# A fused DFT mixing and attention kernel: the seventh PSUM bank as one tile, 17 columns in every value product, and another order of two matmuls in the slots

## The chip, the cores and the metric

The kernel runs on one core of a Trainium2 chip. A core has a matrix engine (TensorE, PE in the profile; its weight loads are listed apart as PEld), a vector engine (VectorE, DVE), an activation engine (ScalarE, ACT), a general engine (GpSimd, POOL) and a queue engine that issues most of the transfers here (SyncE, SP). Matmul results land in PSUM, eight banks of 128 partitions by 512 float32 values. Each engine takes its instructions in the order of its own queue, and engines wait for each other with semaphores. The metric is the device time of one execution in microseconds; the number that counts is the median of the runs.

## What is computed

```python
def reference(A_x, A_dft_seq_re, A_dft_seq_im, A_dft_hid_re, A_dft_hid_im, B_x, B_wqkv, B_wo, gate_w):
    def _A_ref(x, dft_seq_re, dft_seq_im, dft_hid_re, dft_hid_im):
        a = jnp.einsum("bsd,ed->bse", x, dft_hid_re)
        b = jnp.einsum("bsd,ed->bse", x, dft_hid_im)
        y = jnp.einsum("ts,bse->bte", dft_seq_re, a) - jnp.einsum("ts,bse->bte", dft_seq_im, b)
        return y

    def _B_ref(x, wqkv, wo):
        B, S, D = x.shape
        H = 32; Dh = D // H
        qkv = (lambda x, *d: x.transpose(*d))((x @ wqkv).reshape(B, S, 3, H, Dh), 2, 0, 3, 1, 4)
        q, k, v = qkv[0], qkv[1], qkv[2]
        scale = Dh ** -0.5
        scores = jnp.einsum("bhqd,bhkd->bhqk", q, k) * scale
        p = _softmax(scores, axis=-1)
        o = jnp.einsum("bhqk,bhkd->bhqd", p, v)
        return (lambda x, *d: x.transpose(*d))(o, 0, 2, 1, 3).reshape(B, S, D) @ wo

    x = A_x
    g = _sigmoid((x * gate_w).sum(-1, keepdims=True))
    a = _A_ref(x, A_dft_seq_re, A_dft_seq_im, A_dft_hid_re, A_dft_hid_im)
    b = _B_ref(x, B_wqkv, B_wo)
    return g * a + (1 - g) * b
```

There are 2048 tokens of 512 values and 32 heads of 16 values. The projections and the attention use the same x as the DFT branch, and all values are float32. The softmax subtracts the row maximum of the scores, so each score matrix is made twice here: once for its maxima, once for its exponentials.

## The kernel before

The work on PE falls into products of four kinds. The dense ones (projections, the two DFTs, the output projection) are split into a high and a low part of each operand, so that one float32 product is three products of the faster type. They accumulate in one bank named d. A dense product contracts over 128 rows; the kernel cuts it into two **half products** of 64 rows each, issued in line 469 through `Chain.mm`. A **maxima product** (`a_tile`, line 292, letter a) makes one 128 x 512 block of scores with queries on the partitions; DVE reduces it to the maxima of its rows (line 294). A **score product** (`scores`, line 795, letter s) makes a block with keys on the partitions, and ACT takes its exponential into the tile pt (line 796). Both contract over 64 rows, so a half product in one half of the array's rows can run beside a score or maxima product in the other half. A **value unit** (`pv`, line 843) is four products of pt with 16 value columns and a column of ones, each into 32 of the 128 partitions of one bank, the sums acc. The value products are plain float32, and the trace shows each of them as two records.

`segment` writes a stretch of PE's queue from a pattern, a string of slots. A slot such as `a5` puts a maxima product into bank 5, with a half product of the dense work in the other row half; `|` is a value unit. In this kernel the order of every queue is the order of the program, since the schedule is manual. Three patterns matter: THIN (the DFT along the hidden axis, 26 segments), FULL (the DFT along the sequence, 192 segments of 16 slots and two value units) and NINE (the output projection, 26 segments). Segments come in twos: the first issues the lower rows of 16 dense products, the second the upper rows of the same 16.

Banks: seven are numbered. s and a products rotate over banks 0 to 5 by the digits of the pattern; bank 6 holds the sums acc, and between two sums it also takes a product (`s6` in slot 5 and `a6` in slot 11 of FULL). The last value unit of a segment closes the sum (`close`): ACT copies acc to SBUF (`evacuate`, line 822) and POOL adds the copy to the running total (line 823). Before the change, the bank is then given up and a new tile acc is made by the next value unit, whose products take 32 columns so that all partitions of the new tile are written.

In slot 0 of a FULL segment the s or a product stands ahead of the half product in PE's queue (`first`); in the 15 other slots it stands behind it. A half product that opens a segment waits for the reader of the product in the last slot of the segment before, through `users`, which each half product empties.

Of the kernel before, what the change touches and what calls it, by code (L numbers as in the profile page):

```python
# [9 lines left out]
F32 = mybir.dt.float32  # L10
# [5 lines left out]
P = 128  # L16
# [6 lines left out]
NT = S // P  # L23
# [8 lines left out]
def mix_kernel(ctx: ExitStack, tc: tile.TileContext, xa_t, xa, wqkv, w_hid, w_seq, wo, gate_w, out):  # L32
# [5 lines left out]
    nc = tc.nc  # L38
# [29 lines left out]
    psO = Ring(6)  # L68
# [31 lines left out]
    acc = psO.tile([P, 512], F32, "acc")  # L100
# [86 lines left out]
    def bank():  # L187
        nonlocal banks
        banks += 1
        return (psS if banks % 2 else psA).tile([P, 512], F32, name="s" if banks % 2 else "a")  # L190


    with tc.tile_pool(name="qk", bufs=1, reuse_waits="tile") as pool:
# [38 lines left out]
        for tb in range(4):  # L232
# [4 lines left out]
            for c in range(2):  # L237
                if tb == 0 and c == 0:
                    pss = [bank() for _ in range(4)]
                    for kt in range(KT):  # L240
                        x = xab[tb][:, :, :, kt * P:(kt + 1) * P]
# [8 lines left out]
                for ct in range(4):  # L250
                    ps = bank()
# [34 lines left out]
    def a_tile(i, h, ps=None, bank=None):  # L286
        p, j = divmod(i, 64)
        qt, kb = divmod(j, 4)
        if ps is None:
            ps = psA.tile([P, 512], F32, "a", bank)  # L290
        r = slice(64 * h, 64 * h + (64 if p else 48))
        nc.tensor.matmul(ps, qs[p % 2][r, qt * P:(qt + 1) * P], ks[p % 2][r, kb * 512:(kb + 1) * 512],  # L292
                         start=True, stop=True)
        user = nc.vector.tensor_reduce(mx[p % 2][:, h, qt, kb:kb + 1], ps, AX.X, ALU.max)  # L294
        hf = j // 32
        a_left[p, hf] = a_left.get((p, hf), 64) - 1
        if not a_left[p, hf]:
            deferred.extend((partial(m_parts, p, hf), partial(m_rows, p, hf)))
        return user
# [111 lines left out]
    for s in range(8):  # L411
        ps = psS.tile([P, 512], F32, name="s")
# [369 lines left out]
    def scores(u, qb, h, bank=(psS, "s"), number=None):  # L782
        p, r = divmod(u, 32)
        hf, kt = divmod(r, 16)
        q0 = hf * 1024 + qb * 512
        if u >= UNITS - 16:

            blk, kt = divmod(kt, 8)
            q0, kt = 1024 + blk * 512, 2 * kt + qb
        if u not in pts:  # L790
            pts[u] = work.tile([P, 4, 512], F32, name="pt", bufs=4)
        pool, name = bank
        ps = pool.tile([P, 512], F32, name=name) if number is None else pool.tile([P, 512], F32, name, number)
        rr = slice(64 * h, 64 * h + (64 if p else 50))
        nc.tensor.matmul(ps, ks[p % 2][rr, kt * P:(kt + 1) * P], qs[p % 2][rr, q0:q0 + 512], start=True, stop=True)  # L795
        return nc.scalar.activation(pts[u][:, 2 * qb + h], ps, AF.Exp, bias=0.0, scale=DH ** -0.5)  # L796

    def pv_last(u):
        blk, k2 = divmod(u - UNITS + 16, 8)
        pt = pts.pop(u)  # L800
        for j in range(4):
            x, h = divmod(j, 2)
            nc.tensor.matmul(acc[32 * j:32 * j + 17], vt[:, 2 * k2 + x, NP - 1, 16 * h:16 * h + 17], pt[:, j],
                             start=k2 == 0, stop=k2 == 7)
        if blk == 0 and k2 == 7:
            last_pairs.append(LastPair(0, [(psS, "s"), (psA, "a")]))
            last_pairs[0].copy(1)

    part = []

    def evacuate(p, hf, done):

        nonlocal total
        if total is None:
            total = work.tile([P, 512], F32, name="oe", bufs=2)
            nc.scalar.copy(total, acc)
        else:
            if not part:
                two = work.tile([P, 2, 512], F32, name="part", tag="w15")
                part.extend(two[:, i] for i in range(2))  # L820
            part.reverse()
            nc.scalar.copy(part[0], acc)  # L822
            nc.gpsimd.tensor_tensor(total, total, part[0], ALU.add)  # L823
        if done:
            for qb in range(2):
                nc.sync.dma_start(o_d[hf][p, :, qb * 512:(qb + 1) * 512], total[64 * qb:64 * qb + 64])
            total = None

    def pv(u, close=False):
        nonlocal acc  # L830
        if u >= UNITS - 16:
            return pv_last(u)
        p, r = divmod(u, 32)
        hf, kt = divmod(r, 16)
        pt = pts.pop(u)
        begin, done, width = acc is None or kt == 0, kt == NT - 1, 17
        if acc is None:
            acc = psO.tile([P, 512], F32, "acc")
            width = 32
        v = vt.rearrange("p t n d -> p (t n d)")[:, 33 * (NP * kt + p):]  # L840
        for j in range(4):
            h = j % 2
            i = nc.tensor.matmul(acc[32 * j:32 * j + width], v[:, 16 * h:16 * h + width], pt[:, j],  # L843
                                 start=begin, stop=done or close)
        if done or close:
            evacuate(p, hf, done)
            if close:
                acc = None
        return i

    def take(gen, n, whole=True):
# [12 lines left out]
    def issue(x, half, stop=True):  # L864
        chain, st, mv, after, last = x
        i = chain.mm(st, mv, half, last and stop)
        if stop and after:
            after()
        return i
# [15 lines left out]
    for hf in range(2):  # L885
        for ct in range(4):
            n = 3 if hf and ct == 3 else 4
# [32 lines left out]
    FULL = "a5 s4 a2 s0 a3 s6 a5 s4 s1 s0 s2 a6 a3 a4 s5 a1 | |"  # L920
# [15 lines left out]
    users, valued, exponentials = [], 0, []  # L936

    def score(kind, h, number=None):
        x = next(streams[h][kind == "a"], None)
        if x:  # L940
            users.append((kind, a_tile(*x, bank=number) if kind == "a" else scores(*x, number=number)))
            if kind == "s":
                exponentials.append(users[-1][1])

    def values(close=False):
        nonlocal valued
        i = pv(valued, close)
        valued += 1
        return i

    def segment(pattern, half, ds, stop):


        nonlocal users, full_now
        full_now = pattern == FULL
        before, users = users, []
        ds, turned = iter(ds), False
        for n, slot in enumerate(pattern.split()):
            number, other = None, None
            if slot[1:2].isdigit():  # L960
                number, other = int(slot[1]), int(slot[3]) if slot[2:] else None
                slot = slot[::2]
            first = not n and pattern == FULL
            if slot == "|":
                end = n == len(pattern.split()) - 1
                i = values(end)
                if end and pattern == FULL:

                    tc.add_manual_dep(i.ins, exponentials[-2].ins.name,
                                      mybir.DependencyInfo(mybir.DependencyClass.Sync, mybir.DependencyReason.DATA))  # L970
                while between:
                    between.pop(0)()
                if deferred and pattern in NINE and not turned and "|" in pattern.split()[n + 1:]:
                    deferred.pop(0)()
                    turned = True
                continue
            if first:

                score(slot, 1 - half, number)
            if len(slot) == 1:  # L980
                x = next(ds, None)
                if x:

                    before = before if x[0].begun else None
                    i = issue(x, half, stop)
                    users = []
                    if before:
                        tc.add_manual_dep(
                            i.ins, dict(reversed(before)).get("s", before[0][1]).ins.name,
                            mybir.DependencyInfo(mybir.DependencyClass.Sync, mybir.DependencyReason.DATA))  # L990
                        before = None
            if slot != "-" and not first:
                score(slot[-1] if slot[0] == "+" else slot[0], 1 - half, number)
            if len(slot) == 2 and slot[0] != "+":
                score(slot[1].lower(), half, other)

        while full_now and deferred:
            deferred.pop(0)()
        if deferred and not (pattern in NINE and (turned or len(deferred) == 1)):
            deferred.pop(0)()  # L1000
# [11 lines left out]
    first = proj(0, (0, 1, 2), one * 5 + two[:1] + one, range(7))  # L1012
# [5 lines left out]
    pump(hid, 12)  # L1018
    ds = take(hid, 12)
    segment(START[0], 0, ds, False)  # L1020
    pump(hid, 12)
    segment(START[1], 1, ds, True)
    values()
    values(True)
    for patterns, ds in pairs():
        for half in range(2):
            run_plan(valued)
            pattern = FULL if patterns is FULL else patterns[half]
# [5 lines left out]
    for bank in (*three[:1], *three):  # L1034
        scores(*next(streams[1][0]), bank)
# [62 lines left out]
```

## Time and profile before

| | |
|---|---|
| median of 3 runs | 1665.3 us (1664.87 to 1665.42) |
| the profiled execution | 1664.94 us, span 1663.0 us |
| stage of the projections | 0 to 206 us |
| THIN segments | 206 to 353 us |
| FULL segments | 353 to 1458 us |
| NINE segments | 1458 to 1600 us |
| rest | 1600 to 1663 us |

The busy part of the page tells how long each engine worked and how many instructions it had. The chain of waits follows the work that ended last back through the program. Groups put together instructions of one line, engine and shape, with count, busy time, mean duration in nanoseconds, and the idle time ahead of them. The timeline lists instructions by start (us from the start of the span), duration in us, engine, line, operation, output <- inputs, shape and count; instructions of one kind that overlap are merged into one row. In a shape such as 64*128 64x512, the first pair is the rows and columns of the array in use, the second the operand that moves through it.

### The profile page before, as it was taken

Reading aid. Unit: us, or ns where it says so; the run is one execution under the profiler, and the core shown is the slowest. Engines: PE = TensorE matmul, PEld = TensorE weight load, DVE = VectorE, ACT = ScalarE, POOL = GpSimd, SP = SyncE. Lnnn points to the kernel's source line nnn. Section 1 sums busy time; section 2 is a strip of 40 time slices with the busy share of each in tenths; the row PEclk is TensorE's granted clock in tenths of the full one; section 3 lists DMA queues with packets and bytes.
Section 4 is the critical chain, followed back from the end, with each engine's and each line's share of the span. In section 5 each row is a group of like instructions: output and inputs, shape, how many; then the busy total and the mean of one; then the engine's idle time right before and its main releaser. Section 6 shows DMA issues by size and latency. Waiting matters only on the chain.

```text
span 1663.0 us, 34370 instructions
## 1 busy us (share of the span) xinstructions
PE 1655.0 (100%) x13040; PEld 1008.6 (61%) x13040; DVE 1382.6 (83%) x2361; ACT 1266.0 (76%) x2469; POOL 653.5 (39%) x615
## 2 busy tenths in 40 slices
PE   9999999999999999999999999999999999999998
PEld 7888855556566656665666656665566556644443
DVE  5439888888888888888888888888888888899954
ACT  5212388888888888888788888888788878889996
POOL 0202133443434455444343455544444456333330
PEclk9999999999999999999999999999999999999999
DMA  9973610414151343414157534315141535462114
GB/s 295 349 158 120 180 15 9 70 34 85 44 93 47 73 112 81 94 46 79 47 90 254 93 114 96 88 56 90 52 85 59 112 103 122 139 188 40 37 32 140
DMA packets 85245, 167.13 MB, mean 100 GB/s; under 512 B 22461, under 2 KB 22717, under 8 KB 81069
## 3 DMA queue, kind: packets, MB, share of 16 engines
q1 hardware_dynamic: 84648, 164.30, 39.5%
q8 instruction: 102, 1.67, 0.5%
q10 hardware_dynamic: 432, 0.66, 0.1%
q14 instruction: 63, 0.51, 0.1%
HBM read 109.67 MB, written 55.17 MB: 99 GB/s over the span
## 4 chain that ended last, share of the span: by engine, by line
PE 98%; DMA 1%; DVE 0%; POOL 0%; SPq 0%; issue 0%; DVEq 0%; ACT 0%; POOLq 0%; ACTq 0%
PE acc L843 28%; PE d L469 24%; PE a L292 17%; PE s L795 16%; PE s L383 3%; PE s L415 1%; PE d L383 1%; PE a L108 1%; PE s L108 1%; PE s L107 1%; PE a L107 1%; PE a L109 1%; PE s L109 1%; PE a L469 1%; PE s L469 0%; PE s L244 0%
## 5 line engine op out<-in xcount | busy, mean ns | idle before, releaser
L294 DVE TENSOR_REDUCE mx<-a 128x1 f32<-128x512 f32 x2026 | 1260.1, 683 | 172.8 <-PE a L292 144.5
L796 ACT ACTIVATE pt<-s 128x512 f32<-128x512 f32 x2006 | 1021.9, 623 | 33.7 <-PE s L795 17.6
L292 PE MATMUL a<-ks,qs 64*128 64x512 f32 (+1 forms) x2026 | 723.6, 407 | 0.0
L795 PE MATMUL s<-qs,ks 64*128 64x512 f32 (+1 forms) x2006 | 663.9, 395 | 1.0 <-DVE on L736 0.8
L469 PE MATMUL d<-xab,ch 64*128 64x512 f32 x2016 | 644.7, 394 | 0.0
L823 POOL TENSOR_TENSOR oe<-oe,part 128x512 f32<-128x512 f32 x215 | 278.0, 1293 | 660.5 <-ACT part L822 655.5
L292 PEld LDWEIGHTS a<-ks,qs 64*128 64x128 f32 (+1 forms) x2026 | 361.0, 184 | 212.3 <-issue 123.3
L843 PE MATMUL acc<-pt,vt 128*17 128x512 f32 (+1 forms) x3968 | 487.2, 599 | 0.0
L795 PEld LDWEIGHTS s<-qs,ks 64*128 64x128 f32 (+1 forms) x2006 | 361.4, 184 | 71.3 <-ACT pt L796 27.3
L469 PE MATMUL d<-xab,cl 64*128 64x512 f32 x1008 | 397.6, 394 | 0.0
L469 PEld LDWEIGHTS d<-xab,ch 64*128 64x128 f32 x2016 | 366.6, 184 | 28.0
L822 ACT COPY part<-acc 128x512 f32<-128x512 f32 x215 | 126.1, 587 | 187.2 <-PE acc L843 186.2
L843 PEld LDWEIGHTS acc<-pt,vt 128*17 128x17 f32 (+1 forms) x3968 | 92.9, 102 | 218.3 <-issue 138.9
L469 PEld LDWEIGHTS d<-xab,cl 64*128 64x128 f32 x1008 | 185.7, 184 | 14.3
L454 POOL TENSOR_TENSOR cl<-craw,ch 128x512 fp32r<-128x512 f32 x126 | 162.2, 1287 | 10.1
L469 PE MATMUL d<-wre,xab 64*128 64x512 f32 x336 | 90.3, 402 | 0.0
L469 PEld LDWEIGHTS d<-wre,xab 64*128 64x128 f32 x336 | 59.9, 184 | 40.2 <-issue 12.1
L453 POOL CAST ch<-craw 128x512 fp32r<-128x512 f32 x126 | 77.0, 611 | 17.3 <-PE s L795 10.2
L469 PE MATMUL d<-wo_hl,o_hl 64*128 64x512 f32 (+1 forms) x246 | 65.3, 397 | 0.0
L103 ACT CAST hl<-s 128x512 fp32r<-128x512 f32 x28 | 16.1, 587 | 58.4 <-PE s L383 31.3
L469 PEld LDWEIGHTS d<-wo_hl,o_hl 64*128 64x128 f32 (+1 forms) x246 | 44.2, 185 | 16.3 <-ACT pt L796 10.2
L383 PE MATMUL s<-wch,xab 64*128 64x512 f32 x192 | 41.3, 391 | 0.0
(171 smaller groups left out, 992.7 us busy)
## 6 DMA issues: line engine op xcount, KB each, us to landing
craw<-w_seq SPq DMA_DIRECT2D x128, 256.0 KB
qk<-hl SPq DMA_DIRECT2D x32, 512.0 KB
qs<-qk SPq DMA_DIRECT2D x96, 128.0 KB
ks<-qk SPq DMA_DIRECT2D x96, 128.0 KB
b<-hl SPq DMA_DIRECT2D x16, 512.0 KB
xab<-b SPq DMA_DIRECT2D x16, 512.0 KB
o<-oe SPq DMA_DIRECT2D x62, 128.0 KB
oh<-nh SPq DMA_DIRECT2D x12, 512.0 KB
```

The lines of the kernel that those rows point to most:

```text
L107: nc.tensor.matmul(ps, sh, mh, start=first, stop=False)
L292: nc.tensor.matmul(ps, qs[p % 2][r, qt * P:(qt + 1) * P], ks[p % 2][r, kb * 512:(kb + 1) * 512], start=True, stop=True)
L294: user = nc.vector.tensor_reduce(mx[p % 2][:, h, qt, kb:kb + 1], ps, AX.X, ALU.max)
L383: i = nc.tensor.matmul(ps, st[r], mv[r], start=not half and not j, stop=half == 1 and j == 11)
L453: nc.gpsimd.tensor_copy(h1, raw)
L454: nc.gpsimd.tensor_tensor(l1, raw, h1.bitcast(F32), ALU.subtract)
L469: i = nc.tensor.matmul(self.ps, st[r], mv[r], start=not self.begun, stop=stop)
L795: nc.tensor.matmul(ps, ks[p % 2][rr, kt * P:(kt + 1) * P], qs[p % 2][rr, q0:q0 + 512], start=True, stop=True)
L796: return nc.scalar.activation(pts[u][:, 2 * qb + h], ps, AF.Exp, bias=0.0, scale=DH ** -0.5)
L822: nc.scalar.copy(part[0], acc)
L823: nc.gpsimd.tensor_tensor(total, total, part[0], ALU.add)
L843: i = nc.tensor.matmul(acc[32 * j:32 * j + width], v[:, 16 * h:16 * h + width], pt[:, j], start=begin, stop=done or close)
```

## The change

All products into bank 6, also those of slots 5 and 11, now go to the one tile acc that is made at the start of the kernel. No new tile is made behind a closed sum, so every value product takes 17 columns; a flag `closed` tells the next value unit to begin a new sum. Partitions 17 to 31 of each 32 in acc then keep what the last s or a product left, and the copy takes them along; no later step uses them. In FULL segments the s or a product of slots 0 to 14 is issued ahead of the slot's half product; slot 15 keeps the half product first.

```diff
--- before.py
+++ after.py
@@ -790,7 +790,10 @@
         pool, name = bank
-        ps = pool.tile([P, 512], F32, name=name) if number is None else pool.tile([P, 512], F32, name, number)
+        if number == 6:
+            ps = acc
+        else:
+            ps = pool.tile([P, 512], F32, name=name) if number is None else pool.tile([P, 512], F32, name, number)
@@ -806,7 +809,7 @@
-    part = []
+    part, closed = [], False
@@ -827,25 +830,22 @@
     def pv(u, close=False):
-        nonlocal acc
+        nonlocal closed
...
-        begin, done, width = acc is None or kt == 0, kt == NT - 1, 17
-        if acc is None:
-            acc = psO.tile([P, 512], F32, "acc")
-            width = 32
+        begin, done = closed or kt == 0, kt == NT - 1
+        closed = False
         v = vt.rearrange("p t n d -> p (t n d)")[:, 33 * (NP * kt + p):]
         for j in range(4):
             h = j % 2
-            i = nc.tensor.matmul(acc[32 * j:32 * j + width], v[:, 16 * h:16 * h + width], pt[:, j],
+            i = nc.tensor.matmul(acc[32 * j:32 * j + 17], v[:, 16 * h:16 * h + 17], pt[:, j],
                                  start=begin, stop=done or close)
         if done or close:
             evacuate(p, hf, done)
-            if close:
-                acc = None
+            closed = close
         return i
@@ -938,7 +938,7 @@
-            users.append((kind, a_tile(*x, bank=number) if kind == "a" else scores(*x, number=number)))
+            users.append((kind, a_tile(*x, acc if number == 6 else None, number) if kind == "a" else scores(*x, number=number)))
@@ -960,7 +960,7 @@
-            first = not n and pattern == FULL
+            first = pattern == FULL and n < 15
```

On PE, the start of a FULL segment before the change: slots 0 to 5, with what each waits for (the names are output <- operands; L292 is a maxima, L795 a score, L469 a half product).

```order
L292 MATMUL a<-ks_975,qs_973 128x512 [waits Activation_49]
L469 MATMUL d<-xab_205,cl 128x512 [waits DVE_49]
L469 MATMUL d<-xab_205,ch 128x512
L795 MATMUL s<-qs_973,ks_975 128x512
L469 MATMUL d<-xab_205,ch 128x512
L292 MATMUL a<-ks_975,qs_973 128x512
L469 MATMUL d<-xab_205,cl 128x512
L795 MATMUL s<-qs_973,ks_975 128x512
L469 MATMUL d<-xab_206,ch 128x512
L292 MATMUL a<-ks_975,qs_973 128x512
L469 MATMUL d<-xab_206,ch 128x512
L795 MATMUL s<-qs_973,ks_975 128x512 [waits Activation_49]
```

The same place after the change (lines have moved by 3, and the score of slot 5 writes acc):

```order
L292 MATMUL a<-ks_974,qs_972 128x512 [waits Activation_49]
L469 MATMUL d<-xab_203,ch 128x512 [waits DVE_49]
L798 MATMUL s<-qs_973,ks_975 128x512
L469 MATMUL d<-xab_203,ch 128x512
L292 MATMUL a<-ks_974,qs_972 128x512
L469 MATMUL d<-xab_203,cl 128x512
L798 MATMUL s<-qs_973,ks_975 128x512
L469 MATMUL d<-xab_203,ch 128x512
L292 MATMUL a<-ks_974,qs_972 128x512
L469 MATMUL d<-xab_203,ch 128x512
L798 MATMUL acc<-qs_973,ks_975 128x512 [waits Activation_49]
L469 MATMUL d<-xab_203,cl 128x512
```

From slot 1 on, each pair has changed places; slot 0 is as it was.

The end of a FULL segment on PE before, slots 13 to 15 and the two value units:

```order
L469 MATMUL d<-xab_206,ch 128x512
L292 MATMUL a<-ks_975,qs_973 128x512 [waits Activation_49]
L469 MATMUL d<-xab_206,ch 128x512
L795 MATMUL s<-qs_973,ks_975 128x512 [waits DVE_49]
L469 MATMUL d<-xab_206,cl 128x512
L292 MATMUL a<-ks_975,qs_973 128x512 [waits Activation_49]
L843 MATMUL acc<-pt,vt 32x512 [waits DVE_49]
L843 MATMUL acc<-pt,vt 32x512 x3
L843 MATMUL acc<-pt,vt 17x512 x3
L843 MATMUL acc<-pt,vt 17x512 [waits Activation_49]
```

And after:

```order
L292 MATMUL a<-ks_974,qs_972 128x512 [waits Activation_49]
L469 MATMUL d<-xab_204,ch 128x512
L798 MATMUL s<-qs_973,ks_975 128x512 [waits DVE_49]
L469 MATMUL d<-xab_204,cl 128x512
L469 MATMUL d<-xab_204,ch 128x512
L292 MATMUL a<-ks_974,qs_972 128x512 [waits Activation_49]
L844 MATMUL acc<-pt,vt 17x512 [waits DVE_49]
L844 MATMUL acc<-pt,vt 17x512 x6
L844 MATMUL acc<-pt,vt 17x512 [waits Activation_49]
```

In slots 13 and 14 the waiting product now stands ahead of the half product of its slot, slot 15 is as before, and all value products take 17 columns. The order on DVE, POOL and SP is the same as before, and so is that on ACT, where the copy of the sums has a wait more:

```order
L822 COPY part<-acc 128x512 [waits PE_49,Pool_49]
L796 ACTIVATE pt<-s 128x512 [waits PE_49] x4
L796 ACTIVATE pt<-s 128x512 [waits PE_49,Activation_49]
L796 ACTIVATE pt<-s 128x512 [waits PE_49]
L796 ACTIVATE pt<-s 128x512 [waits PE_49,Activation_49]
```

```order
L825 COPY part<-acc 128x512 [waits DVE_49,PE_49,Pool_49]
L799 ACTIVATE pt<-s 128x512 [waits PE_49] x2
L799 ACTIVATE pt<-acc 128x512 [waits PE_49]
L799 ACTIVATE pt<-s 128x512 [waits PE_49]
L799 ACTIVATE pt<-s 128x512 [waits PE_49,Activation_49]
```

The first of these two is before the change, the second after it: the copy of the sums, then exponentials of the next segment.

## The prediction

> **What bounds the kernel now.** I read the page first: the busy shares and the chain that ended last.
>
> ```profile
> span 1663.0 us, 34370 instructions
> PE 1655.0 (100%) x13040; PEld 1008.6 (61%) x13040; DVE 1382.6 (83%) x2361; ACT 1266.0 (76%) x2469; POOL 653.5 (39%) x615
> PE 98%; DMA 1%; DVE 0%; POOL 0%; SPq 0%; issue 0%; DVEq 0%; ACT 0%; POOLq 0%; ACTq 0%
> ```
>
> TensorE (PE) is busy for the whole span and 98% of the chain is its own work, so a nanosecond that it gains in every segment is kept, as long as VectorE (DVE) and ScalarE (ACT) follow. The stage that the change edits most comes next, from the busy time by stretches: columns are PE, weight loads, DVE, ACT and POOL.
>
> ```profile
> 353.00:1458.00 1105.00, 1105.00 (x9224) 669.19 (x9216) 972.97 (x1664) 901.01 (x1762) 508.92 (x474) 1.00 0.39 90
> ```
>
> These 1105 us hold the 192 FULL segments, 5.755 us each. DVE works 88% of them and ACT 82%, so both can follow a PE that becomes a few tenths of a per cent faster. The granted clock is 1.00 throughout. I therefore look at what a segment's 5.755 us consist of, in PE's order of time, for one of average length.
>
> ```profile
> 698.76 0.50 PE L292 MATMUL a<-ks,qs 64*128 64x512 f32 x1
> 698.76 0.50 PE L469 MATMUL d<-xab,ch 64*128 64x512 f32 x1
> 699.09 0.39 PE L795 MATMUL s<-qs,ks 64*128 64x512 f32 x1
> 699.10 0.39 PE L469 MATMUL d<-xab,ch 64*128 64x512 f32 x1
> ...
> 700.02 0.39 PE L795 MATMUL s<-qs,ks 64*128 64x512 f32 x1
> ...
> 700.71 0.39 PE L469 MATMUL d<-xab,cl 64*128 64x512 f32 x1
> 700.71 0.39 PE L795 MATMUL s<-qs,ks 64*128 64x512 f32 x1
> ...
> 701.40 0.39 PE L292 MATMUL a<-ks,qs 64*128 64x512 f32 x1
> ...
> 701.64 0.39 PE L292 MATMUL a<-ks,qs 64*128 64x512 f32 x1
> ...
> 702.10 0.39 PE L795 MATMUL s<-qs,ks 64*128 64x512 f32 x1
> 702.30 0.39 PE L469 MATMUL d<-xab,ch 64*128 64x512 f32 x1
> 702.33 0.39 PE L292 MATMUL a<-ks,qs 64*128 64x512 f32 x1
> 702.65 1.92 PE L843 MATMUL acc<-pt,vt 128*32 128x512 f32 x16
> 704.51 0.49 PE L292 MATMUL a<-ks,qs 64*128 64x512 f32 x1
> ```
>
> The two row halves of the array work side by side: a half product d in one, a score or maxima product (I call both s here) in the other. Sixteen slots take 698.76 to 702.65, the two value units 702.65 to 704.51, and the next segment follows without a gap. Two things matter. In slot 1 the program issues d before s, and yet s starts first (699.09 against 699.10): the halves start on their own, whatever the order of issue. And from slot 8 on (700.71) d leads: seven steps later it is at 702.30, a step of 0.227 us, while s is at 702.33, a step of 0.231. The value units need all rows, so the later stream, s, sets their start.
>
> **Part 1: 17 columns in every value product.** Each first value unit behind a closed sum has four products of 32 columns, and the trace shows each in two passes. The groups with shapes kept apart:
>
> ```profile
> L843 PE MATMUL acc<-pt,vt 128*17 128x512 f32 x2008 | 261.4, 593 | 0.0
> L843 PE MATMUL acc<-pt,vt 128*32 128x512 f32 x1960 | 261.1, 605 | 0.0
> ```
>
> 1960 records are 1960 / 8 = 245 units. A wide product is 12 ns longer in the mean (605 against 593). That this is time of the stream, and not a longer overlap, is seen where a wide and a narrow unit stand alone between slots, in the stage ahead of the FULL segments:
>
> ```profile
> 313.01 1.05 PE L843 MATMUL acc<-pt,vt 128*17 128x512 f32 x8
> 314.00 0.49 PE L469 MATMUL d<-wre,xab 64*128 64x512 f32 x1
> ...
> 316.49 1.06 PE L843 MATMUL acc<-pt,vt 128*32 128x512 f32 x8
> 317.49 0.50 PE L292 MATMUL a<-ks,qs 64*128 64x512 f32 x2
> ```
>
> The narrow unit takes 0.99 us to the next slot, the wide one 1.00. So the term is 245 x 0.012 = 2.9 us gained. Its bounds are 0 (the rounded rows could hide a step of almost nothing) and 245 x 0.02 = 4.9 (the most that they allow).
>
> **Part 2: one tile for the seventh bank.** DVE, POOL and SP issue the same instructions in the same order, and the matmuls of this bank wait as before. What is new is that the copy of the sums on ACT waits for DVE too, because it now reads rows that the maxima product of slot 11 wrote. The value units ahead of that copy have waited for the same reduction already:
>
> ```profile
> 701.85 0.69 DVE L294 TENSOR_REDUCE mx<-a 128x1 f32<-128x512 f32 x1
> ...
> 702.65 0.15 PEld L843 LDWEIGHTS acc<-pt,vt 128*32 128x32 f32 x7 [0.31 <-DVE mx L294]
> ```
>
> The reduction ends at 702.54, 0.11 us ahead of the value units, and the copy comes behind them. I cost this at nothing. The 0.11 us is also the room by which the slots may shrink before DVE becomes the gate; and as that reduction starts when slot 11's product is done (701.40 + 0.39 = 701.79), it moves along with a faster PE. If ACT took time to test a third wait, it would be part of the last rival's cost.
>
> **Part 3: s ahead of d in slots 1 to 14.** Nothing is added: 14 pairs a segment swap places, in 192 segments. What can change is who leads. The row to compare with is a segment in which s stays ahead by chance:
>
> ```profile
> 1331.57 0.49 PE L292 MATMUL a<-ks,qs 64*128 64x512 f32 x1
> ...
> 1333.29 0.39 PE L795 MATMUL s<-qs,ks 64*128 64x512 f32 x1
> 1333.30 0.39 PE L469 MATMUL d<-xab,cl 64*128 64x512 f32 x1
> ...
> 1334.88 0.39 PE L795 MATMUL s<-qs,ks 64*128 64x512 f32 x1
> 1334.90 0.39 PE L469 MATMUL d<-xab,ch 64*128 64x512 f32 x1
> 1335.11 0.39 PE L292 MATMUL a<-ks,qs 64*128 64x512 f32 x1
> 1335.12 0.39 PE L469 MATMUL d<-xab,ch 64*128 64x512 f32 x1
> 1335.44 1.92 PE L843 MATMUL acc<-pt,vt 128*32 128x512 f32 x16
> 1337.29 0.50 PE L292 MATMUL a<-ks,qs 64*128 64x512 f32 x1
> ```
>
> From slot 7 to slot 14 the leading s steps by 0.227 us and the following d by 0.229, both reach slot 15 within 0.01, and from its start to the next segment's it takes 5.72 us where the average one took 5.75. That is 0.03 x 192 = 5.8 us, the upper bound of this part. s falls behind where it must wait for a bank, as its weight loads show:
>
> ```profile
> 700.03 0.18 PEld L292 LDWEIGHTS a<-ks,qs 64*128 64x128 f32 x1
> ...
> 701.67 0.18 PEld L292 LDWEIGHTS a<-ks,qs 64*128 64x128 f32 x1
> ...
> 702.16 0.18 PEld L292 LDWEIGHTS a<-ks,qs 64*128 64x128 f32 x1
> ```
>
> A load normally starts with the product before it. The load for slot 6 comes about 0.01 us late (700.03 against the product of slot 5 at 700.02), that for slot 13 0.03 late (701.67 against 701.64), that for slot 15 0.06 late (702.16 against 702.10). Slot 6 is where d passes s today, because d's loads stand ahead of the waiting one. With s first, d's load of the same slot is queued behind that wait, and d gets no free pass. What is queued behind a waiting s is now that d and all later products; the value units wait for both streams. But a load has room: for slot 15 it starts 0.17 us ahead of its product (702.16 to 702.33), where a full step is 0.23, and that product still came on time, so a load 0.06 late costs nothing. The waits of slots 6 and 13 lie within that. The low bound is therefore 0 when the waits still let the two streams drift apart, and, if the room were not there, a loss of (0.01 + 0.03) x 192 = 7.7 us. Slot 15, with the longest wait, keeps d first. I take half of the upper bound, 2.9 us: s will lead more often, but it is s that waits, and a segment led by s is nearer to what the swap makes than one in which d is held 0.04.
>
> The Trainium skill, in "TensorE: Matmul & The Clock Gate", section "The mechanism", says that matmuls start strictly in program order and only weight loads are pulled ahead. The pair at 699.09 and 699.10 speaks against this, since s started ahead of the d issued before it. By that rule d could never start ahead of its slot's s after the swap, but s would keep its own step of 0.231, the segment would end where it ends now, and only part 1 would be left, the time of the first rival.
>
> **The sum.** -2.9 (columns) + 0 (tile) - 2.9 (order) = -5.8 us. The profiled execution took 1664.94 us, of which the span is 1663.0; with 5.8 less it is 1659.1. The median of the runs, 1665.3, is 0.4 above that execution, which gives 1659.5.
>
> **The rivals.** (a) The order does nothing, since the halves start on their own and s is slow by its own waits, not by d. For it: slot 1 above. Against it: the leader's step is 0.227 in both segments, whichever stream leads. Time: 1665.3 - 2.9 = 1662.4. (b) The order gives all of its bound: s leads in nearly every segment, as at 1331.57. Against it: the waits of slots 13 and 15 remain, and a shorter slot stage makes ACT's releases later by comparison. Time: 1665.3 - 2.9 - 5.8 = 1656.6. (c) Slower: PE's queue stands behind s. At slots 6 and 13 s waits for DVE and ACT, d's load stands behind it and both halves idle, 0.04 us a segment that d's lead absorbed before. It decides where d's load starts more than 0.06 us after the product before it; then the time is 1665.3 - 2.9 + 7.7 = 1670.1. For it: DVE and ACT are 88% and 82% busy and the waits do occur in every segment. Against it: the room of 0.06 us, and the one segment led by s that shows no such loss.
>
> **How the numbers follow.** The forecast of 1659.5 has a chance of 0.4, (a) 0.28, (b) 0.2, (c) 0.12. About 0.2%, 3.3 us, is what a measurement of this kernel can tell from no change: that puts the line at 1662.0. (a) lies just on the other side of it, so it goes to the same side but for a small part; faster is 0.4 + 0.2 and I leave it at 0.6, same 0.28, slower 0.12. The range takes in (b) with 1 us below it and the near half of the way from no change to (c): 1655.5 to 1667. The likeliest case alone would be 1658 to 1661.
>
> **What would show it.** Part 1: no group of 32 columns is left, and the two units take 0.01 us less than the 1.86 us above (702.65 to 704.51). Part 2: ACT's copy starts no later behind the value units than before. Part 3: in most segments s starts ahead of d in the late slots, the step of s falls to 0.227 to 0.229, and the value units start less than 3.89 us after the segment's start. The forecast is wrong if the late d products start more than 0.03 behind s (then the lag has only changed sides), if d's loads at slots 6 and 13 come more than 0.06 late, or if the value units' loads start right at the end of the reduction of slot 11.

## The result and the profile after

The change takes 3.4 us off: 1661.83 us median (1661.07 to 1662.97, 17 runs) against 1665.26 us before (1664.09 to 1666.32, 17 runs). The ratio is 0.998, 95% interval 0.9973 to 0.9987. The forecast was 1659.5 in a range of 1655.5 to 1667; the time of the first rival, the columns without any gain from the order, was 1662.4.

The page of the profiled execution after the change, which took 1662.97 us:

```profile
span 1661.1 us, 34392 instructions
PE 1651.7 (99%) x13040; PEld 976.0 (59%) x13040; DVE 1383.3 (83%) x2361; ACT 1264.7 (76%) x2469; POOL 654.0 (39%) x615
PE 98%; DMA 1%; DVE 0%; POOL 0%; SPq 0%; ACT 0%; issue 0%; DVEq 0%; POOLq 0%; ACTq 0%
```

PE is still 98% of the chain. The groups, with shapes kept apart, hold one form of value product now, and ACT sat idle ahead of the copy of the sums, which has a third wait now, as long as before (185.7 us; the last row is that of before, 187.2 us). In the FULL segments the copy starts 0.137 us behind the recorded end of the last value product in the median, against 0.148 before:

```profile
L844 PE MATMUL acc<-pt,vt 128*17 128x512 f32 x3968 | 484.1, 596 | 0.0
L825 ACT COPY part<-acc 128x512 f32<-128x512 f32 x215 | 126.4, 588 | 185.7 <-issue 174.6 <-POOL cl L454 5.7 <-PE acc L844 5.1
```

```profile
L822 ACT COPY part<-acc 128x512 f32<-128x512 f32 x215 | 126.1, 587 | 187.2 <-PE acc L843 186.2 <-POOL ch L453 0.6
```

PE's timeline for a FULL segment of the length that most have after the change:

```profile
687.61 0.49 PE L292 MATMUL a<-ks,qs 64*128 64x512 f32 x1
687.61 0.49 PE L469 MATMUL d<-xab,cl 64*128 64x512 f32 x1
...
688.87 0.40 PE L798 MATMUL acc<-qs,ks 64*128 64x512 f32 x1
688.88 0.40 PE L469 MATMUL d<-xab,ch 64*128 64x512 f32 x1
...
689.57 0.39 PE L798 MATMUL s<-qs,ks 64*128 64x512 f32 x1
689.58 0.39 PE L469 MATMUL d<-xab,ch 64*128 64x512 f32 x1
...
691.18 0.39 PE L292 MATMUL a<-ks,qs 64*128 64x512 f32 x1
691.18 0.39 PE L469 MATMUL d<-xab,cl 64*128 64x512 f32 x1
691.50 1.91 PE L844 MATMUL acc<-pt,vt 128*17 128x512 f32 x16
693.35 0.49 PE L292 MATMUL a<-ks,qs 64*128 64x512 f32 x1
```

The value units take 1.85 us (691.50 to 693.35; 1.86 before). The order did what it says: s (score or maxima product) leads and d (half product) follows within 0.01 us up to slot 15 (691.18), where s was 0.03 behind before. Yet the sixteen slots take 3.89 us (687.61 to 691.50), as in the average segment before. From slot 8 to slot 15 the leading s needs 691.18 - 689.57 = 1.61, a step of 0.230; before, the leading d had 0.227. The lead of d is gone, and s has kept its pace. The prediction's other signs of being wrong did not come: the loads of the value units start 0.11 us behind the end of the reduction of slot 11 in the median (0.09 before), and d's loads of slots 6 and 13 start 0.014 and 0.010 us behind the product before them in the mean.

The rounded rows hide differences of a few ns, so I took the unrounded starts of the matmuls in the traces, one execution of each kernel, over all 192 FULL segments, and averaged. "Slots" is from a segment's first product to its first value product, "values" from there to the next segment, "lag" is how far s starts behind d in slot 15, "FULL" the time from the first segment's start to the last one's, in us like the rest. The experiments below are in the same table.

```
kernel                        slots    values   lag     FULL
before                        3.899    1.854    0.031   1098.87
after                         3.896    1.842   -0.001   1095.96
columns alone                 3.903    1.842    0.035   1097.13
order alone                   3.896    1.854    0.001   1098.37
half product first            3.918    1.842    0.051   1100.14
d first in 6, 13, 15          3.900    1.842    0.032   1096.55
maxima over 256               3.878    1.842   -0.003   1092.48
exponentials of 256           3.898    1.842   -0.004   1096.30
both of 256                   3.857    1.842   -0.005   1088.45
other banks                   3.879    1.842   -0.004   1092.57
other banks, old order        3.888    1.842    0.021   1094.25
other banks, d first in 13    3.875    1.842    0.008   1091.82
```

FULL gained 2.9 us: 191 x 0.0127 = 2.4 in the value units and 191 x 0.0025 = 0.5 in the slots. Another 0.4 us came in the THIN stage and behind FULL. The spans differ by 1.9 us only, because the profiled execution after the change reached the first dense product of line 107 1.3 us later (at 17.64 us against 16.30), ahead of any edited instruction.

### The profile page after: what moved, and what is told of

It is laid out like the page before. It is cut to its first block, busy times and chain, and to the rows that moved or that the text cites. A ratio compares the mean times of both kernels' runs of the same rounds, so it can differ in the third digit from the quotient of the medians.

```text
span 1661.1 us, 34392 instructions
## 1 busy us (share of the span) xinstructions
PE 1651.7 (99%) x13040; PEld 976.0 (59%) x13040; DVE 1383.3 (83%) x2361; ACT 1264.7 (76%) x2469; POOL 654.0 (39%) x615
## 4 chain that ended last, share of the span: by engine, by line
PE 98%; DMA 1%; DVE 0%; POOL 0%; SPq 0%; ACT 0%; issue 0%; DVEq 0%; POOLq 0%; ACTq 0%
PE acc L844 28%; PE a L292 21%; PE s L798 19%; PE d L469 12%; PE s L383 3%; PE acc L798 3%; PE acc L292 2%; PE s L415 1%; PE d L383 1%; PE a L108 1%; PE a L107 1%; PE s L108 1%; PE s L107 1%; PE a L109 1%; PE s L109 1%; PE a L469 1%
## 5 line engine op out<-in xcount | busy, mean ns | idle before, releaser
L294 DVE TENSOR_REDUCE mx<-a 128x1 f32<-128x512 f32 x1834 | 1144.1, 683 | 158.3 <-PE a L292 115.0
L799 ACT ACTIVATE pt<-s 128x512 f32<-128x512 f32 x1762 | 933.2, 624 | 32.8 <-PE s L798 17.3
L292 PE MATMUL a<-ks,qs 64*128 64x512 f32 (+1 forms) x1834 | 679.3, 409 | 0.0
L469 PE MATMUL d<-xab,ch 64*128 64x512 f32 x2016 | 647.8, 396 | 0.0
L798 PE MATMUL s<-qs,ks 64*128 64x512 f32 (+1 forms) x1762 | 574.1, 395 | 0.9 <-DVE on L736 0.5
L844 PE MATMUL acc<-pt,vt 128*17 128x512 f32 x3968 | 484.1, 596 | 0.0
L292 PEld LDWEIGHTS a<-ks,qs 64*128 64x128 f32 (+1 forms) x1834 | 325.6, 184 | 231.9 <-issue 122.5
L469 PE MATMUL d<-xab,cl 64*128 64x512 f32 x1008 | 399.3, 396 | 0.0
L469 PEld LDWEIGHTS d<-xab,ch 64*128 64x128 f32 x2016 | 366.5, 184 | 11.5
L798 PEld LDWEIGHTS s<-qs,ks 64*128 64x128 f32 (+1 forms) x1762 | 316.1, 184 | 80.5 <-ACT pt L799 28.2
L825 ACT COPY part<-acc 128x512 f32<-128x512 f32 x215 | 126.4, 588 | 185.7 <-issue 174.6
L844 PEld LDWEIGHTS acc<-pt,vt 128*17 128x17 f32 x3968 | 86.7, 96 | 224.2 <-issue 141.8
L469 PEld LDWEIGHTS d<-xab,cl 64*128 64x128 f32 x1008 | 185.6, 184 | 5.9
L294 DVE TENSOR_REDUCE mx<-acc 128x1 f32<-128x512 f32 x214 | 147.8, 691 | 10.7
L799 ACT ACTIVATE pt<-acc 128x512 f32<-128x512 f32 x244 | 147.9, 606 | 0.0
L798 PE MATMUL acc<-qs,ks 64*128 64x512 f32 (+1 forms) x244 | 95.4, 391 | 0.0
L469 PE MATMUL d<-wre,xab 64*128 64x512 f32 x336 | 90.5, 402 | 0.0
L469 PEld LDWEIGHTS d<-wre,xab 64*128 64x128 f32 x336 | 59.9, 184 | 40.7 <-issue 12.3
L292 PE MATMUL acc<-ks,qs 64*128 64x512 f32 (+1 forms) x214 | 83.1, 388 | 0.0
```

Source lines behind the costliest of these rows:

```text
L469: i = nc.tensor.matmul(self.ps, st[r], mv[r], start=not self.begun, stop=stop)
L844: i = nc.tensor.matmul(acc[32 * j:32 * j + 17], v[:, 16 * h:16 * h + 17], pt[:, j], start=begin, stop=done or close)
```

## Experiments: columns and order apart

The first two runs separate the parts. Columns alone is the kernel after the change with the old order:

```diff
-            first = pattern == FULL and n < 15
+            first = not n and pattern == FULL
```

> One tile and 17 columns, with the order of before (score or maxima product first in slot 0 alone). Theory A (the change is worth its columns: 0.0128 us in each of 192 FULL segments and about as much in 53 others, 3.1 us; the order is worth the 0.5 us of the slots in the profile after): 3.1 us below before, value units 1.842 us a segment as after, slots 3.90 us as before, with the half product ahead in the late slots. Theory B (the order carries the gain, and the columns lie under another wait): less than 1 us below before.

Measured: 1662.71 us against 1665.76 in the same job, ratio 0.9983 (0.9974 to 0.9991), 3.05 us below. Theory A holds, B falls.

Order alone is the kernel before, with the opposite edit.

> The order of the change (slots 0 to 14 score or maxima first), with a new tile and 32 columns as before. Theory A: 0.5 us below before, value units 1.854 us, slots 3.896 us, both streams within 0.01 us of each other in the late slots. Theory B: about 3 us below before.

Measured: 1664.81 us, ratio 0.9994 (0.9985 to 1.0003), 0.95 us below and not told apart from no change by the interval. The lag went from 0.031 to 0.001 and the slots from 3.899 to 3.896: the order does move the lead, and the lead is worth next to nothing. By FULL, in one execution each, the order is worth 0.5 us with 32 columns (1098.87 to 1098.37) and 1.2 us with 17 (1097.13 to 1095.96).

The half product first everywhere:

```diff
-            first = pattern == FULL and n < 15
+            first = False
```

> One tile, 17 columns, and the half product first in all 16 slots, slot 0 too. If the order of issue only decides which stream may pass a wait (theory A), the half products lead by 0.03 us in the late slots as before, the slots take 3.90 us, and the time is that of the columns alone, 3.1 us below before. If the product issued first in slot 0 sets the lead and the pace of the segment (theory C), the half products lead from slot 0 on, run at 0.227 us a slot, and the score stream falls further back: slots over 3.92 us, the time less than 0 to 1 us below before.

Measured: 1666.55 us, ratio 1.0005 (0.9996 to 1.0013), 0.8 us above before: the gain of the columns is lost again. In the means this looks like theory C: slots of 3.918 (it asked for over 3.92), s 0.019 us behind d in slot 0 and 0.051 in slot 15. But the means mix two kinds of segments. In 180 of the 192, s starts 0.003 to 0.004 behind d in slot 0, and their slots take 3.905, as with the columns alone. In the 12 others, every sixteenth, s starts 0.10 to 0.42 behind, and the slots take 4.116. In these, three or four separate wait instructions of line 292, some 0.1 us apart, come ahead of the segment's first maxima product. With the columns alone they are over 0.9 us ahead of slot 0. Here they stand behind the half product, which waits for the reduction of the segment before; the last of them starts between 0.01 us ahead of that product and 0.32 behind it, and s's first load comes 0.07 to 0.39 behind it. These twelve make 12 x (4.116 - 3.905) = 2.5 us of the 3.0 by which FULL is longer than with the columns alone. So by these times most of the loss is not that d leads and sets the pace, as theory C has it, but that other waits queue behind a waiting d.

Score first, except in the slots whose loads come late:

```diff
-            first = pattern == FULL and n < 15
+            first = pattern == FULL and n not in (6, 13, 15)
```

> One tile, 17 columns, score or maxima product first in slots 0 to 14 except 6 and 13, whose loads come late in the profiles, so that the half product's load no longer stands behind those waits. If the waits ahead of the half products' loads hold the streams at 0.230 us a slot (theory D), the half products' loads at slots 6 and 13 are on time, slots fall below 3.88 us and the time to 4 to 6 us below before. If those waits lie within the room of a load (theory A), time and slots as after the change, 3.4 us below before.

Measured: 1662.39 us, ratio 0.998 (0.9971 to 0.9989), 3.4 us below. d's loads in slots 6 and 13 are on time again, and d is back in the lead by 0.032 at the end. In the mean s is 0.004 ahead in slot 5, 0.002 in slot 6 and 0.003 behind in slot 7, so slot 6 is where d passes it, as the prediction read it. But slots (3.900) and time are those of the kernel after, so theory D falls. Whether d waits with s or not changes next to nothing here, because s sets the end either way.

## Experiments: what holds the step of s

Leading does not make s faster. So either something slows s itself, or 0.230 is the step of such a pair. Three kernels take waits for banks away by leaving out half of the work of the engines that release them, and one tests the operands.

```diff
-        user = nc.vector.tensor_reduce(mx[p % 2][:, h, qt, kb:kb + 1], ps, AX.X, ALU.max)
+        user = nc.vector.tensor_reduce(mx[p % 2][:, h, qt, kb:kb + 1], ps[:, :256], AX.X, ALU.max)
```

> The kernel after the change, with each row maximum taken over 256 of the 512 columns (half of the reduction is left out), so that VectorE releases its banks earlier and reads half as much of PSUM. Theory E (the score stream's step of 0.230 us comes from its waits for banks and from the readers of the banks): the waits for VectorE at slots 6 and 14 and ahead of the value units go, the step falls towards 0.227, slots below 3.87 us, 4 us or more below the kernel after. Theory F (0.230 is the step of two row halves that are fed with alternating products, whoever reads them): slots stay at 3.89 to 3.90 us and the time within 1 us of the kernel after.

```diff
-            pts[u] = work.tile([P, 4, 512], F32, name="pt", bufs=4)
+            pts[u] = fixed[u % 4]
...
-        return nc.scalar.activation(pts[u][:, 2 * qb + h], ps, AF.Exp, bias=0.0, scale=DH ** -0.5)
+        return nc.scalar.activation(pts[u][:, 2 * qb + h, :256], ps[:, :256], AF.Exp, bias=0.0, scale=DH ** -0.5)
```

The four tiles `fixed` are set to 1 once, ahead of the attention; the third kernel has both edits.

> The kernel after the change, with exponentials of 256 of the 512 columns (the other half of each block of pt stays at 1, from fixed tiles set once), so that ScalarE releases its banks earlier. Theory E: the late loads of slots 13 and 15 (0.012 and 0.036 us late in the mean after the change) come on time, the step falls towards 0.227, slots below 3.87 us, 4 us or more below the kernel after. Theory F: loads on time, yet slots at 3.89 to 3.90 us and the time within 1 us of the kernel after.

> Both of the above: maxima over 256 columns and exponentials of 256 columns are left out by half, so that no product waits for a bank. Theory E: slots about 3.83 us (336 + 14 x 227 + 320 ns), 12 us below the kernel after. Theory F: slots 3.88 to 3.90 us, within 2 us of the kernel after.

Measured: 1659.32 us with short maxima (ratio 0.9962, 0.9948 to 0.9976), 1663.45 with short exponentials (0.9984, 0.9975 to 0.9994), 1650.83 with both (0.9912, 0.9897 to 0.9926). In the first and the third the slots do fall, to 3.878 and 3.857, and the times are 3.0 and 11.5 us further below before than that of the kernel after. That is against theory F, but both slots are longer than theory E asked (below 3.87, and 3.83): the steps 2 to 6 behind the value units stay long. In the second the loads of slots 13 and 15 do come on time, as E asks, and slots stay at 3.898, as F asks. Its ten runs spread the most (1660.42 to 1665.59), and the profiled one, 1661.54, is among the quickest. What that second kernel has left is one late load, that of slot 6, and this makes the pair with the third kernel the clearest view of the study. The s products of slots 5 to 10 on PE with short exponentials, and the two loads of slot 6:

```profile
631.27 0.40 PE L801 MATMUL acc<-qs,ks 64*128 64x512 f32 x1
...
631.51 0.39 PE L292 MATMUL a<-ks,qs 64*128 64x512 f32 x1
...
631.75 0.39 PE L801 MATMUL s<-qs,ks 64*128 64x512 f32 x1
...
631.98 0.39 PE L801 MATMUL s<-qs,ks 64*128 64x512 f32 x1
...
632.22 0.38 PE L801 MATMUL s<-qs,ks 64*128 64x512 f32 x1
...
632.44 0.39 PE L801 MATMUL s<-qs,ks 64*128 64x512 f32 x1
```

```profile
631.29 0.18 PEld L292 LDWEIGHTS a<-ks,qs 64*128 64x128 f32 x1
631.29 0.18 PEld L469 LDWEIGHTS d<-xab,ch 64*128 64x128 f32 x1
```

The same with both halved:

```profile
491.52 0.39 PE L801 MATMUL acc<-qs,ks 64*128 64x512 f32 x1
...
491.75 0.39 PE L292 MATMUL a<-ks,qs 64*128 64x512 f32 x1
...
491.98 0.39 PE L801 MATMUL s<-qs,ks 64*128 64x512 f32 x1
...
492.20 0.39 PE L801 MATMUL s<-qs,ks 64*128 64x512 f32 x1
...
492.43 0.39 PE L801 MATMUL s<-qs,ks 64*128 64x512 f32 x1
...
492.66 0.39 PE L801 MATMUL s<-qs,ks 64*128 64x512 f32 x1
```

```profile
491.52 0.18 PEld L292 LDWEIGHTS a<-ks,qs 64*128 64x128 f32 x1
491.53 0.18 PEld L469 LDWEIGHTS d<-xab,ch 64*128 64x128 f32 x1
```

With both halved, the loads of slot 6 start with the product of slot 5 (491.52), and the products of slots 6 to 10 take 492.66 - 491.75 = 0.91, four steps of 0.227. With short exponentials alone the loads start 0.02 us behind the product (631.29 against 631.27). The product of slot 6 itself starts hardly later for it (a step of 0.24, 631.27 to 631.51, where the other kernel has 491.75 - 491.52 = 0.23), but the four steps behind it take 632.44 - 631.51 = 0.93. The unrounded means over the segments of the steps of s show how it goes on, in ns:

```
step into slot                6     7     8     9     10    11    12    13    14    15
after                        232   231   232   230   228   230   229   230   231   233
maxima over 256              230   230   228   228   228   227   227   229   231   233
exponentials of 256          235   234   233   233   226   231   233   229   231   229
both of 256                  230   228   227   227   227   227   227   227   227   227
other banks                  230   229   228   228   228   227   227   229   231   232
```

Long steps follow a late load. Where the late loads are those of slots 13 and 15 (maxima over 256, and the other banks of the next section), the long steps are at the end; where it is that of slot 6 alone (exponentials of 256), they begin there and go on to slot 15, with one of 226 among them; where there is none, all steps from slot 8 on are 227. A load on time starts 3 ns behind the product before it; the one of slot 6, in both streams, starts 14 behind in the median. It is the one load whose time differs between the second and the third kernel, and their slots are 41 ns apart, 3.898 and 3.857.

The cost does not grow with the delay. In the kernel with short exponentials, the 172 segments in which s's load of slot 6 starts 13 to 16 ns behind the product have slots of 3.901 in the mean; the 13 in which it starts more than 16 behind have 3.866, and the 5 with 12 have 3.862.

```diff
-        nc.tensor.matmul(ps, qs[p % 2][r, qt * P:(qt + 1) * P], ks[p % 2][r, kb * 512:(kb + 1) * 512],
+        nc.tensor.matmul(ps, ks[p % 2][r, qt * P:(qt + 1) * P], qs[p % 2][r, kb * 512:(kb + 1) * 512],
```

> The kernel after the change, with the maxima products computed from ks as the stationary and qs as the moving operand, as the score products are (their blocks are then not the maxima's). The score stream no longer changes its operands' roles from slot to slot. If that alternation costs the step (theory G), the step falls to 0.227 and slots to about 3.84 us; if not (E or F), slots stay at 3.89 to 3.90 us. The maxima now read columns that a transfer has just written, so single segments may wait for it; the median segment decides.

Measured: 1780.02 us, ratio 1.0686 (1.067 to 1.0702); PE waits 100.6 us for the transfer that the expectation names. In the 178 segments whose slots take less than 4.0 us, the mean is 3.895 and the steps of s from slot 9 on are 229 to 231, much as in the kernel after. Theory G falls.

## Experiments: the late load taken away with all work done

Slot 6 waits because it takes bank 5, which slot 0 used. Bank 1 was last used by slot 15 of the segment before. If the two change places from one segment to the next, slot 6 always finds a bank that has been read since:

```diff
-    FULL = "a5 s4 a2 s0 a3 s6 a5 s4 s1 s0 s2 a6 a3 a4 s5 a1 | |"
+    FULL = ("a5 s4 a2 s0 a3 s6 a1 s4 s5 s0 s2 a6 a3 a4 s1 a5 | |",
+            "a1 s4 a2 s0 a3 s6 a5 s4 s1 s0 s2 a6 a3 a4 s5 a1 | |")
...
-            pattern = FULL if patterns is FULL else patterns[half]
+            pattern = patterns[half]
```

> The kernel after the change, with banks 1 and 5 changing places from segment to segment (slots 0, 6, 8, 14, 15), so that slot 6 takes a bank that has been free since the segment before; the same work, in the same order. Theory H (a load that comes late by as little as 0.014 us does not delay its own product, but makes the four or five steps behind it longer, in whichever row half it stands): the late load of slot 6 goes in both streams, steps 7 to 11 fall to 0.227 to 0.228, slots to 3.87 to 3.88 us, the time to 3 to 4 us below the kernel after, 1658 to 1659. If a late load costs no more than the room allows (theory A), slots stay at 3.896 us and the time at 1661.8 to 1662.4.

Measured: 1660.02 us against 1665.38, ratio 0.9968 (0.9956 to 0.9981), 5.4 us below before. Slots fell to 3.879, and FULL is 3.4 us shorter than after the change (1095.96 to 1092.57), as theory H asks. The load of slot 6 starts with the product of slot 5 now, and the four steps behind slot 6 take 808.18 - 807.27 = 0.91, as with both halved:

```profile
807.04 0.39 PE L798 MATMUL acc<-qs,ks 64*128 64x512 f32 x1
...
807.27 0.39 PE L292 MATMUL a<-ks,qs 64*128 64x512 f32 x1
...
808.18 0.39 PE L798 MATMUL s<-qs,ks 64*128 64x512 f32 x1
```

```profile
807.04 0.18 PEld L292 LDWEIGHTS a<-ks,qs 64*128 64x128 f32 x1
807.04 0.18 PEld L469 LDWEIGHTS d<-xab,ch 64*128 64x128 f32 x1
```

All of the reductions are done here, and yet the slots and the steps of s are those of short maxima (3.878) within 0.001 us, so what halving the reductions gave there is accounted for by this one load. The time missed the 1658 to 1659 of the expectation by 1 us. The median gained 1.9 us on the change's 3.4; in the profiled execution, the slowest of the five, the part behind FULL took 2.3 us longer than in that of before, and why stays open. So a load that hardly delayed its own product had cost 3.4 us of FULL.

The same banks with the old order:

> The same banks with the order of before (half product first in slots 1 to 15). Theory H: without the late load of slot 6 no stream falls behind there; the score stream keeps its 0.003 us lead up to slot 13, and the time is within 1 us of the run with the order of the change. If the order has a worth of its own, 2 us or more between the two.

Measured: 1661.62 us, ratio 0.9978 (0.9969 to 0.9987). Without the late load of slot 6, s stays within 0.004 us of d up to slot 12, nearly as expected (its lead of 0.003 shrinks from slot 3 on and is gone by slot 9); from slot 13 on, whose load starts 0.038 us behind the product before it, s falls back, to 0.021 behind in slot 15. FULL is 1.7 us longer than with the new order and the median 1.6, which lies between the two expectations, so whether the order has a small worth of its own at slot 13 stays open.

And with the half product first in slot 13:

```diff
-            first = pattern in FULL and n < 15
+            first = pattern in FULL and n < 15 and n != 13
```

> The same banks, score or maxima first in slots 0 to 14 but for 13, so that the half product's load does not stand behind the late load of slot 13. Theory H: only the maxima stream has long steps behind slot 13, and as it sets the end, the time is that of the first of these three kernels within 0.5 us.

Measured: 1658.98 us, ratio 0.9961 (0.9947 to 0.9974), 6.4 us below before and 1.0 below the kernel without this edit; in FULL it is 0.8 us. The expectation, the same time within 0.5, is missed by that. This is the fastest kernel that does all the work. The end of a segment of its profile:

```profile
408.69 0.39 PE L292 MATMUL a<-ks,qs 64*128 64x512 f32 x1
408.70 0.39 PE L469 MATMUL d<-xab,ch 64*128 64x512 f32 x1
408.92 0.39 PE L469 MATMUL d<-xab,cl 64*128 64x512 f32 x1
408.93 0.39 PE L292 MATMUL a<-ks,qs 64*128 64x512 f32 x1
...
409.38 0.39 PE L469 MATMUL d<-xab,ch 64*128 64x512 f32 x1
409.39 0.39 PE L292 MATMUL a<-ks,qs 64*128 64x512 f32 x1
409.72 1.91 PE L844 MATMUL acc<-pt,vt 128*17 128x512 f32 x16
```

Both streams still start within 0.01 us of each other in slots 12 to 15, so neither waits long for the other ahead of the value units. Which stream has the long steps is plain in the means: d, whose load of slot 13 is on time now, steps by 227 in slots 13 to 15, where it stepped by 229 to 231 in the kernel without this edit, and s, whose load is late in both, by 230 to 232.

## Why the prediction was right, and where it was not

The time fell into the range with one of its two terms nearly missing: 1661.83 lies nearer to the first rival (1662.4) than to the forecast (1659.5).

**The bound** was right: PE was and is 98% of the chain, and what its stages gained came out at the end.

**The columns** were right in size: 2.9 us forecast, 3.05 measured alone. That a wide unit holds the stream longer is right too: 12.7 ns a segment in FULL, and unrounded the two kinds of unit in THIN take 0.996 and 0.983 us to the next slot. But of the two readings, the one from the group means came out by luck. Only the first four of a wide unit's eight records were long in FULL before, 617 ns, and the other four took 592, as all eight of the narrow unit behind it. After the change the first four of the same unit still take 604. So the 12 ns between the groups are half of 25, of which 13 belong to the width and 12 to the place at the head; the stream gains once a unit, where the second four start 0.441 us behind the first in place of 0.453 (medians over FULL).

**The tile** at nothing was right: the copy's idle time did not grow, and columns alone, which has the tile as well, lost nothing to it.

**The order** is the term that failed. It was put at 2.9 us, half of a bound of 5.8; it measured 0.5 to 1.2. Two steps led there. The first took a segment in which s happened to lead (1331.57) as the picture of what the swap makes, and read "the leader has 0.227" as a rule. The swap put s ahead all through slots 9 to 14 in 157 of the 192 segments, where it was 10 before, and the leader then had 0.230. That one segment was short for another reason, as the trace has it. Its load of slot 6 started 18 ns behind the product of slot 5 (1332.85 against 1332.83), and before the change the 35 segments with that load more than 16 behind have slots of 3.881 in the mean, though s leads at the end in only 7 of them; the 103 with 13 to 16 behind have 3.898. Why the exact delay matters, and why d took the long steps in that segment although s's load was the late one, stays open. The second step is "a load 0.06 late costs nothing". The product of such a load is indeed next to on time, but the steps behind it are longer, and the late loads of slots 6, 13 and 15 together kept s at 0.230 in both orders: with that of slot 6 alone on time and the same work, slots fell from 3.896 to 3.879, with none late, and half of the reductions and exponentials left out, to 3.857. The part of the text that held slot 6 to be the place where d passes s was right: with d first in slots 6 and 13, d passes s behind slot 6 again.

**The rivals.** The first, that the order does nothing, was nearly the outcome (1662.4 against 1661.83), with its reason half right: s is slow by its own waits, though by their after-effect more than by their length. The third, that the queue stands behind s, did not come: d's loads in slot 6 started 14 ns behind the product with s's, and the slots were no longer for it (3.896 against 3.899).

**The rule** of the Trainium skill ("TensorE: Matmul & The Clock Gate", section "The mechanism") that matmuls start in program order was weighed and set aside for the pair at 699.09 and 699.10. The runs agree with setting it aside: with the other banks and d issued first in slots 1 to 15, s still starts 2 to 4 ns ahead of d in slots 1 to 4 in the mean.

## What to carry to other kernels

When two streams run side by side and one ends later, ask what slows that one; letting it lead does not help if its own waits set its pace. A weight load that starts late can cost time even where its own product starts on time, so look at the steps behind it, and give the slot a bank that has been free for longer. A gain that rests on one lucky segment should be checked against what else is different in that segment, and a difference of two group means against where the members of each group stand.

## What the runs showed of the hardware that I had not expected

A load that starts 14 ns behind the product before it, where 3 is usual, makes most steps behind it 2 to 6 ns longer where both row halves' loads are late (short exponentials, slots 7 to 15, against both halved). Where only s's load is late, d's steps are back at 227 in the means (d first in slot 13). Yet there is room between a load and its product: before the change, the load of slot 15 starts 51 ns behind in the mean, for a step of 233. The effect is not one of more delay, more cost (3.901 us with 13 to 16 ns, 3.866 with more). With no late load the step is 227 ns from slot 8 on, while the steps into slots 2 to 6 are 229 to 236 ns in the means of every kernel here but the one with swapped operands; why a break of the stream is followed by long steps stays open.
